# The last stage writes over silu(y) in place; x's first rows come in one load, transposing loads one by one; totals for two weights' scales use a score bank

## The chip, the cores and the metric

The kernel runs on one core of a Trainium2 chip. The core has TensorE for matmuls (its weight loads are shown apart, as PEld), VectorE (DVE), ScalarE (ACT), GpSimd (POOL) and SyncE (SP). In this kernel SyncE issues all DMAs, one after the other. [...] The metric is the device time of one execution in microseconds (us), lower is better.

## The reference

x is 2048 rows of 640 columns. It is normalized by row, and two branches start from the result: sliding-window attention with 32 heads of 20 columns and a window of 256, and an MLP with squared relu and 1536 hidden columns. The output adds x to the product of the attention branch and silu of the MLP branch.

```python
def _A_ref(x, wqkv, wo):
    H = 32; Dh = D // H; W = 256
    qkv = (x @ wqkv).reshape(B, S, 3, H, Dh).transpose(2, 0, 3, 1, 4)
    q, k, v = qkv[0], qkv[1], qkv[2]
    scores = einsum("bhqd,bhkd->bhqk", q, k) * (Dh ** -0.5)
    mask = (idx[:, None] - idx[None, :] >= 0) & (idx[:, None] - idx[None, :] < W)
    p = softmax(where(mask, scores, -1e9))
    o = einsum("bhqk,bhkd->bhqd", p, v)
    return o.transpose(0, 2, 1, 3).reshape(B, S, D) @ wo

def _B_ref(x, w1, b1, w2, b2):
    h = einsum("bsd,df->bsf", x, w1) + b1
    r = where(h > 0, h, 0)
    return einsum("bsf,fd->bsd", r * r, w2) + b2

xn = layernorm(A_x)
out = A_x + _A_ref(xn, A_wqkv, A_wo) * silu(_B_ref(xn, B_w1, B_b1, B_w2, B_b2))
```

(The transposes are written shorter here than in the original; what is computed is the same.)

## The kernel before

**Numbers in two parts.** A float32 operand is split into a float16 high part and a float16 rest, and a product is three matmuls into one PSUM bank: high by high, high by rest, rest by high. Weights are scaled before the split. The scale of a weight comes from its sum of squares: a matmul with a matrix of ones (`totals`, L151) adds over the partitions, a VectorE reduce reads the PSUM result, and a few instructions on single columns (`weight_scale`, L137) make the scale and its inverse.

**Stages.** The first stage normalizes x, turns it (`xT`, four blocks of 512 rows) and makes v. Then 256 steps of attention run: a step is one of 16 pairs of heads (`p`) and one of 16 tiles of 128 rows (`q`). The loop at L1064 has 269 steps, since a step's later parts lag behind: `scores` and `maxima` of step s come with `scores_t` and `exps` of step s-10, `high` of s-11, `low` of s-12 and `values` of s-13. `scores` (L564) fills two banks of tag "s" with up to 320 columns of scores each; the last 128 columns of the first are used every fourth step for a transpose of the row maxima. `maxima` (L577) reads both with VectorE.

**Filler.** Between the parts of a step, `fill` (L1046) takes matmuls from the generator `filler` (L928): the products for the other groups of q and k (`group_unit`, L852), the hidden layer (`hidden_unit`, L877, 8 blocks of 256 rows by 12 groups of 128 columns), the MLP's second product (`out_unit`, L898; `outs` of tag "ysb", stored to `y_d` in DRAM) and at the end the last stage, `out_filler` (L997). All of them take their banks from tag "mm", which has three. `second_scales` (L824) and `out_scales` (L830), the scales of w2 and wo, are called from the filler too; their totals matmul also takes a bank of "mm".

**The last stage.** For each of 8 blocks `u` of 256 rows (two tiles `t` each): `yb` holds y, loaded from `y_d` by `load_y` (L966; two blocks share one buffer of pool `bigp`), and ScalarE makes silu of it in place (L1018). `oT` holds the attention output turned, in two parts, by two transposing loads from `o_d` (`load`, L973), which may start for the blocks 0 and 1 from step 261 on, for 2 and 3 from step 265 on, and for the others when the steps are over. A tile takes two groups of 15 matmuls with wo (`nh`, 320 columns each). `finish` (L998) multiplies the bank by the scale and by silu(y) (L999), adds x (L1000), and after the second group the tile is stored to the output. The result tile `res` has the tag "ysb" with two buffers; that tag is also the one of `outs` in `out_unit`. x's tiles come through `load_res` (L993) into tag "wraw" with three buffers, which the raw pieces of wo use before. A finish runs on VectorE one group later than its matmuls are issued (`pending`, `flush`, L707); stores are collected in `posts` and issued by `post_all` (L696).

**Order.** The order of every engine's instructions, SyncE's DMAs among them, is the order in which this program writes them. A wait of one instruction holds all behind it on the same engine. `bigp` has ten buffers; a new tile takes one whose last users are through.

Of the kernel before, what the change touches and what calls it, by code (L numbers as in the profile page):

```python
# [58 lines left out]
def attn_mlp_kernel(ctx: ExitStack, tc, x, wqkv, wo, w1, b1, w2, b2, out):  # L59
# [69 lines left out]
    def col(name, n=1):  # L129
        return const.tile([P, n], F32, name=name)  # L130
# [19 lines left out]

    def totals(name, r, acc, k=1):  # L151
        nc.tensor.matmul(r, onesf, acc, start=True, stop=True)
        t = col(name, k)
        nc.vector.tensor_reduce(out=t, in_=r.rearrange("p (k n) -> p k n", k=k), op=ALU.add, axis=mybir.AxisListType.X)
        nc.vector.tensor_scalar(t, t, TINY, None, ALU.max)
        return t
# [403 lines left out]
        vps[p] = vp  # L560

    mts = {}

    def scores(p, q, between):  # L564
        i = p % 2
        r = [pat.tile([P, 4 * P], F32, tag="s", name="sps") for h in range(2)]
        rows = between and between(r[0])
        nk = min(WIN + HB, (q + 1) * P)
        for j in range(2):
            q0 = q * P + j * HB  # L570
            k0 = max(0, q0 - WIN)
            for h, ps in enumerate(r):
                rows_ = slice(HB * h, HB * h + HR)
                nc.tensor.matmul(ps[HB * j:HB * (j + 1), :nk], qs[i][rows_, q0:q0 + HB], ks[i][rows_, k0:k0 + nk], start=True, stop=True)  # L574
        return (r, mask if q > 1 else mask0[:, 2 * P - nk:], nk), rows

    def maxima(p, q, r):  # L577
        if q % 4 == 0:
            mts[p, q // 4] = mtp_.tile([P, 8], F32, tag="mt", name="mt")
        mt = mts[p, q // 4]  # L580
        r, mk, nk = r
        for h, ps in enumerate(r):
            junk = mtp_.tile([P, WIN + HB], BF16, tag="junk", name="junk")
            at_ = 4 * h + q % 4
            nc.vector.tensor_tensor_reduce(out=junk[:, :nk], in0=ps[:, :nk], in1=mk, scale=1.0 / MAX_UNIT, scalar=-3.0e38, op0=ALU.add, op1=ALU.max, accum_out=mt[:, at_:at_ + 1])  # L585
        if q % 4 == 3:
            mp = mps[q // 4 % 2]
            v = mp[:, 0:16].rearrange("p (h a b) -> p h a b", h=2, a=2)
            m_ = mt.rearrange("p (h b) -> p h b", h=2)
            nc.gpsimd.tensor_copy(v[:, :, 0, :], m_)  # L590
            nc.gpsimd.tensor_sub(v[:, :, 1, :], m_, v[:, :, 0, :])
            mts[p, q // 4] = mp
# [228 lines left out]
        nc.gpsimd.tensor_mul(g2, ss2, mlp["ic4"])  # L821
        mlp["g2"] = g2

    def second_scales():  # L824
        s2, i2 = weight_scale("w2", totals("w2_t", pmm.tile([P, NF], F32, tag="mm", name="sums2"), mlp["g2"]))
        sf = col("m_sf", NF)
        nc.vector.tensor_scalar(sf, mlp["ic2"], s2, None, ALU.mult)
        mlp.update(s2=sf, i2=i2)

    def out_scales():  # L830
        so, io = weight_scale("wo", totals("wo_t", pmm.tile([P, KC], F32, tag="mm", name="sumso"), sso))
        iw = col("o_inv")
        nc.gpsimd.tensor_mul(iw, io, mlp["iv"])
        nc.gpsimd.tensor_scalar(iw, iw, 1.0 / (XS * V_DOWN), 1.0, ALU.mult, ALU.mult)
        mlp.update(so=so, io=iw)
# [16 lines left out]
    def group_unit(g, b, w):  # L852
        if w == "q":
            if b == 0:
                ensure(f"g{g}")
            if g == 1 and b == 0:
                queue_squares()
            if b == 1 and g + 1 < KC:
                ws[g + 1] = queue_group(g + 1)
            if g == 3 and b == 0:  # L860
                ensure("s")
                weighted_squares()
            if g == 3 and b == 1:
                second_scales()
                for j in range(3):
                    queue_w2(j)
        hi, lo = ws[g][w]
        ps = pmm.tile([P, BT], F32, tag="mm", name="qkps")
        yield from mm_group(ps, [(wt[:, c, :], xT[b][:, part, c, :]) for c in range(KC) for wt, part in ((hi, 0), (hi, 1), (lo, 0))], 0.218)

        def evac():
            hm = stg.tile([P, 2, BT], F16, tag="stg", name="shm")
            qk_parts(hm, ps)
            posts.extend(qk_stores(w, slice(g * P, (g + 1) * P), slice(b * BT, (b + 1) * BT), hm))
        pending.append(evac)
# [51 lines left out]

    def filler():  # L928
        groups = [(group_unit, g, b, w) for g in range(1, KC) for b in range(NB) for w in "qk"]
        hid = [[(hidden_unit, n, fc) for fc in range(NF)] for n in range(nblk)]  # L930
        mlp2 = [[(out_unit, n, tt, nh, third) for tt in range(2) for nh in range(2) for third in range(3)] for n in range(nblk)]
        first = 3 * NB
        units = groups[:first] + merge(groups[first:], hid[0])
        for n in range(nblk - 1):
            units += merge(hid[n + 1], mlp2[n])
        units += mlp2[-1]
        for u in units:
            if u == (hidden_unit, 1, 2):
                out_scales()
            if u[:3] == (hidden_unit, nblk - 1, 0):  # L940
                wo_part = queue_wo()
                for y in range(4):
                    load_y(y)
                shut.add("o")
            if u[:2] == (out_unit, nblk - 1):
                shut.discard("o")
                if u[2:] == (1, 1, 0):
                    ensure("o")
                    load_res(0)
                    load_res(1)  # L950
                for y in range(4, 6):
                    load_y(y)
                for z in range(4):
                    load(z)
            if u == (out_unit, nblk - 1, 1, 1, 2):
                load_y(6)
            yield from u[0](*u[1:])
        ensure("o")
        yield from out_filler(wo_part)
# [30 lines left out]

    xres = {}

    def load_res(t):  # L993
        xres[t] = wgt.tile([P, D], F32, tag="wraw", bufs=RAW, name="xres")
        nc.sync.dma_start(xres[t], x[t * P:(t + 1) * P, :])

    def out_filler(wo_part):  # L997
        def finish(ps, sl, t2, nh, res, xt, t, yb):  # L998
            nc.vector.scalar_tensor_tensor(res[:, sl], ps, mlp["io"], yb[:, t2, sl], ALU.mult, ALU.mult)  # L999
            nc.vector.tensor_add(res[:, sl], res[:, sl], xt[:, sl])  # L1000
            if t == NT - 1:
                post(out[t * P:(t + 1) * P, sl], res[:, sl])
            elif nh:
                post(out[t * P:(t + 1) * P, :], res)

        for u in range(2 * NB):
            while u not in oT:
                load(u)
                if u not in oT:
                    yield None  # L1010
            if u == 0:
                flush()
                post_all()
                load_y(7)
            load(u + 1)
            flush()
            yb = ybs[u]
            nc.scalar.activation(yb, yb, AF.Silu)  # L1018
            for t2 in range(2):
                t = 2 * u + t2  # L1020
                xt = xres.pop(t)
                res = wgt.tile([P, D], F32, tag="ysb", name="res")
                for nh in range(2):
                    sl = slice(nh * HALF, (nh + 1) * HALF)
                    cuts = [sl] if (t, nh) != (NT - 1, 1) else [slice(HALF, HALF + HALF // 2), slice(HALF + HALF // 2, D)]
                    for sl in cuts:
                        ps = pmm.tile([P, HALF], F32, tag="mm", name="wops")[:, 0:sl.stop - sl.start]
                        mms = []
                        for c in range(KC):
                            for op, wp in ((0, 0), (0, 1), (1, 0)):  # L1030
                                mms.append((oT[u][:, op, c, t2 * P:(t2 + 1) * P], wo_part(wp, c)[:, sl]))
                        yield from mm_group(ps, mms, 0.138)
                        if sl is not cuts[-1]:
                            pending.append(lambda ps=ps, sl=sl: finish(ps, sl, t2, nh, res, xt, t, yb))
                    if nh and t + 2 < NT:
                        load_res(t + 2)
                    load(u + 1)
                    load(u + 2)

                    pending.append(lambda args=(ps, sl, t2, nh, res, xt, t, yb): finish(*args))  # L1040

    fl = filler()
    total_ = 8 * (KC - 1) * 15 * 0.218 + 8 * (12 * 15 * 0.111 + 4 * 36 * 0.138)
# [14 lines left out]
    with tc.manual_schedule(engines={E_.PE, E_.Activation, E_.DVE, E_.Pool, E_.SP}):  # L1058
# [5 lines left out]
        for s in range(steps):  # L1064
# [24 lines left out]
            if s % 4 == 1 and 1 < s <= NP * NT + 1:  # L1089
                def between(tp=None, s=s):  # L1090
                    return max_rows((s - 2) // NT, (s - 2) % NT // 4, tp)
# [70 lines left out]
```

## Time and profile before

| | us |
|---|---|
| median of 3 runs | 826.05 (824.84 to 827.02) |
| the profiled execution | 823.97 |
| its span, first to last instruction | 822.2 |
| TensorE busy | 803.9 |
| VectorE busy | 692.4 |
| ScalarE busy | 647.0 |
| GpSimd busy | 496.6 |
| last attention score matmul | about 715 |
| last stage's first matmul | 743.2 |

The profile is one execution. Busy time is that of an engine's own instructions; waiting and DMA issue are not in it. The views used below: the page's shares; the busy time of each engine in chosen stretches of the span (with the clock granted to TensorE, 1.00 is full, the mean busy share of the 16 DMA engines, and what they moved in GB/s); and the timeline of one engine, with start and length of each row in us, the line, the operation, the tiles written and read, their shapes and a count. A bracket at a row's end is the engine's idle time before it and what ended that. SPq is SyncE's queue, where a row is the issue of a DMA and not its transfer. PEld is the loading of matmul weights.

### The profile page before, as it was taken

Reading aid. Unit: us, or ns where it says so; the run is one execution under the profiler, and the core shown is the slowest. Engines: PE = TensorE matmul, PEld = TensorE weight load, DVE = VectorE, ACT = ScalarE, POOL = GpSimd, SP = SyncE. Lnnn points to the kernel's source line nnn. Section 1 sums busy time; section 2 is a strip of 40 time slices with the busy share of each in tenths; the row PEclk is TensorE's granted clock in tenths of the full one; section 3 lists DMA queues with packets and bytes.
Section 4 is the critical chain, followed back from the end, with each engine's and each line's share of the span. In section 5 each row is a group of like instructions: output and inputs, shape, how many; then the busy total and the mean of one; then the engine's idle time right before and its main releaser. Section 6 shows DMA issues by size and latency. Waiting matters only on the chain.

```text
span 822.2 us, 25122 instructions
## 1 busy us (share of the span) xinstructions
PE 803.9 (98%) x9373; PEld 537.0 (65%) x9373; DVE 692.4 (84%) x1943; ACT 647.0 (79%) x1064; POOL 496.6 (60%) x874
## 2 busy tenths in 40 slices
PE   8999999999999999999999999999999999998798
PEld 7775563455555567777777777777777777766476
DVE  6777566898999989999999999999999999982454
ACT  5565455999899989898999999999999999995000
POOL 2000000556687779787888989898897988870000
PEclk9999999999999999999999999999999999999999
DMA  7995358764655522222222222222132261269894
GB/s 249 257 342 165 112 162 263 222 188 123 191 152 151 161 73 55 51 66 67 39 67 60 66 54 68 50 52 70 35 90 52 62 221 41 86 114 201 222 229 158
DMA packets 153250, 104.51 MB, mean 127 GB/s; under 512 B 97192, under 2 KB 127656, under 8 KB 153128
## 3 DMA queue, kind: packets, MB, share of 16 engines
q1 hardware_dynamic: 153128, 102.92, 45.7%
q8 instruction: 73, 1.20, 0.6%
q14 instruction: 49, 0.40, 0.2%
HBM read 60.43 MB, written 36.83 MB: 118 GB/s over the span
## 4 chain that ended last, share of the span: by engine, by line
PE 84%; ACT 6%; DVE 4%; DMA 3%; issue 2%; SPq 1%; ACTq 0%; DVEq 0%
PE hps L718 19%; PE yps L914 19%; PE qkps L718 10%; PE ops L654 8%; PE sps L574 7%; PE wops L718 6%; PE vps L293 6%; PE stps L621 4%; PE qkps L519 3%; ACT p L626 2%; PE tps L257 1%; SPq L980 1%; ACT ph L634 1%; DMA out_dram<-res 1%; DMA y<-ysb 1%
## 5 line engine op out<-in xcount | busy, mean ns | idle before, releaser
L626 ACT ACTIVATE p<-stps,ebias,esc 128x768 f32<-128x768 f32 (+2 forms) x256 | 242.1, 946 | 33.5 <-PE stps L621 16.1
L640 DVE TENSOR_TENSOR pl<-p,ph 128x768 f16<-128x768 f32 (+2 forms) x256 | 247.3, 966 | 2.2 <-ACT ph L634 1.4
L585 DVE CUSTOM_DVE_ANT_0 junk<-sps,mask 128x320 bf16<-128x320 f32 (+2 forms) x512 | 220.4, 466 | 31.3 <-PE sps L574 27.3
L627 POOL TENSOR_SCALAR_AFFINE_SELECT p<-p 128x256 f32<-128x256 f32 x256 | 175.1, 684 | 65.5 <-ACT p L626 57.4
L634 ACT ACTIVATE ph<-p 128x768 f16<-128x768 f32 (+2 forms) x256 | 203.1, 793 | 2.4 <-POOL p L629 1.5
L718 PE MATMUL hps<-xT,w 128*128 128x256 f16 x1440 | 189.5, 273 | 1.0 <-ACT relu L888 1.0
L914 PE MATMUL yps<-w,hh 128*128 128x320 f16 x1152 | 187.1, 300 | 0.0
L718 PEld LDWEIGHTS <-w 128*128 128x128 f16 x1440 | 132.4, 98 | 45.2 <-issue 25.7
L914 PEld LDWEIGHTS <-hh 128*128 128x128 f16 x1152 | 104.8, 98 | 56.2 <-issue 22.5
L718 PE MATMUL qkps<-xT,qkw 128*128 128x512 f16 x480 | 115.5, 380 | 0.0
L629 POOL TENSOR_SCALAR_AFFINE_SELECT p<-p 128x256 f32<-128x256 f32 x224 | 107.0, 478 | 0.0
L654 PE MATMUL ops<-vp,ph 128*128 128x41 f16 x1440 | 89.8, 181 | 0.0
L654 PE MATMUL ops<-vp,pl 128*128 128x41 f16 x1440 | 89.5, 180 | 0.0
L654 PEld LDWEIGHTS <-ph 128*128 128x128 f16 x1440 | 84.6, 96 | 5.1
L574 PE MATMUL sps<-ks,qs 60*64 60x320 f16 (+2 forms) x1024 | 84.0, 313 | 1.7 <-DVE mt L585 1.3
L654 PEld LDWEIGHTS <-pl 128*128 128x128 f16 x1440 | 78.9, 96 | 5.1
L892 POOL TENSOR_TENSOR hh<-sq,hh 128x256 f16<-128x256 f32 x96 | 66.7, 695 | 20.4 <-DVE sq L891 12.2
L621 PE MATMUL stps<-qs,ks 62*64 62x320 f16 (+4 forms) x1024 | 77.5, 290 | 1.0 <-ACT p L626 0.8
L718 PEld LDWEIGHTS <-qkw 128*128 128x128 f16 x480 | 42.4, 98 | 53.7 <-issue 11.5
L590 POOL CAST mp<-mt 128x8 f16<-128x8 f32 x64 | 44.4, 693 | 54.1 <-DVE mt L585 53.4
L718 PE MATMUL wops<-wo,oT 128*128 128x320 f16 (+1 forms) x495 | 67.4, 299 | 7.8 <-DVE res L999 7.8
L293 PE MATMUL vps<-wv,xT 128*128 128x320 f16 x480 | 69.6, 299 | 1.3 <-DVE xT L267 0.4
(150 smaller groups left out, 996.4 us busy)
## 6 DMA issues: line engine op xcount, KB each, us to landing
raw<-in_B_w_dram SPq DMA_DIRECT2D x24, 320.0 KB
ks<-k_d SPq DMA_DIRECT2D x64, 120.0 KB
qs<-q_d SPq DMA_DIRECT2D x64, 120.0 KB
v_d<-vt SPq DMA_DIRECT2D x8, 656.0 KB
vp<-v_d SPq DMA_DIRECT2D x16, 328.0 KB
xt<-in_A_x_dram SPq DMA_DIRECT2D x16, 320.0 KB
k_d<-shm SPq DMA_DIRECT2D x20, 256.0 KB
q_d<-shm SPq DMA_DIRECT2D x20, 256.0 KB
```

What stands on the lines that cost most here:

```text
L293: nc.tensor.matmul(ps, xT[b][:, xp, c, t * P:(t + 1) * P], wv[wp][:, c, nh * HALF:(nh + 1) * HALF], start=n == 0, stop=n == 3 * KC - 1)
L574: nc.tensor.matmul(ps[HB * j:HB * (j + 1), :nk], qs[i][rows_, q0:q0 + HB], ks[i][rows_, k0:k0 + nk], start=True, stop=True)
L585: nc.vector.tensor_tensor_reduce(out=junk[:, :nk], in0=ps[:, :nk], in1=mk, scale=1.0 / MAX_UNIT, scalar=-3.0e38, op0=ALU.add, op1=ALU.max, ...
L621: nc.tensor.matmul(ps[HB * j:HB * (j + 1), hh, c0:c1], ks[i][rows_, kb * P + HB * j:kb * P + HB * (j + 1)], qs[i][rows_, kb * P + c0:kb * ...
L626: nc.scalar.activation(p32[:, :, :n], ps[:, :, :n], AF.Exp, scale=esc[0], bias=ebias)
L627: nc.gpsimd.affine_select(p32[:, :, 0:P], p32[:, :, 0:P], pattern=[[0, 2], [1, P]], compare_op=ALU.is_ge, fill=0.0, base=0, channel_multip ...
L629: nc.gpsimd.affine_select(p32[:, :, 2 * P:], p32[:, :, 2 * P:], pattern=[[0, 2], [-1, P]], compare_op=ALU.is_gt, fill=0.0, base=0, channel ...
L634: nc.scalar.activation(ph[:, :, :n], p32[:, :, :n], AF.Copy)
L640: nc.vector.tensor_sub(pl[:, :, :n], p32[:, :, :n], ph[:, :, :n])
L654: nc.tensor.matmul(ot[:, q % 4, hh, :], t[:, hh, (q - k) * P:(q - k + 1) * P], vp[:, k // 4, k % 4, hh, :], start=m == 1, stop=m == 2 * le ...
L718: nc.tensor.matmul(ps, a, b_, start=j == 0, stop=j == n - 1)
L914: nc.tensor.matmul(ps, hh[:, hp, tt * P:(tt + 1) * P], lin1(w2t, (2 * fc + wp) * D + nh * HALF, HALF), start=fc == 0 and j == 0, stop=fc = ...
```

## The change

Five things change. (1) `finish` writes its result over `yb`, the block that holds silu(y); `res` is now `yb[:, t2]` and no longer a tile of tag "ysb". (2) x's first four tiles come in one load of 512 rows into a buffer of `bigp` (`first_res`), at the start of the last block's second MLP product, instead of four loads of one tile each. (3) From inside the last `out_unit`s only blocks 0 and 1 of `oT` are asked for; in the last stage the block after next is asked for at the second tile of a block only. (4) y's blocks 6 and 7 are loaded at the end of blocks 0 and 1 of the last stage, and the flush and the stores at the start of the stage are left to the usual places. (5) The totals for w2's and wo's scales go into the last 128 columns of the second score bank of the next step: the matmul is issued ahead of that step's scores, and the reduce and what follows it come behind that step's maxima.

```diff
     def totals(name, r, acc, k=1):
         nc.tensor.matmul(r, onesf, acc, start=True, stop=True)
+        return totals_rest(name, r, k)
+
+    def totals_rest(name, r, k=1):
         t = col(name, k)
...
+    sums_due = []
 
     def scores(p, q, between):
         i = p % 2
         r = [pat.tile([P, 4 * P], F32, tag="s", name="sps") for h in range(2)]
         rows = between and between(r[0])
+        sums_rest = sums_due.pop(0)(r[1][:, 3 * P:]) if sums_due else None
...
-        return (r, mask if q > 1 else mask0[:, 2 * P - nk:], nk), rows
+        return (r, mask if q > 1 else mask0[:, 2 * P - nk:], nk, sums_rest), rows
 
     def maxima(p, q, r):
...
+        if sums_rest:
+            sums_rest()
         if q % 4 == 3:
...
-    def second_scales():
-        s2, i2 = weight_scale("w2", totals("w2_t", pmm.tile([P, NF], F32, tag="mm", name="sums2"), mlp["g2"]))
+    def summed(name, acc, rest):
+        def go(r):
+            r = r[:, :acc.shape[-1]]
+            nc.tensor.matmul(r, onesf, acc, start=True, stop=True)
+            return lambda: rest(*weight_scale(name, totals_rest(f"{name}_t", r)))
+        sums_due.append(go)
+
+    def second_scales(s2, i2):
...
-    def out_scales():
-        so, io = weight_scale("wo", totals("wo_t", pmm.tile([P, KC], F32, tag="mm", name="sumso"), sso))
+    def out_scales(so, io):
...
             if g == 3 and b == 1:
-                second_scales()
+                summed("w2", mlp["g2"], second_scales)
...
             if u == (hidden_unit, 1, 2):
-                out_scales()
+                summed("wo", sso, out_scales)
...
             if u[:2] == (out_unit, nblk - 1):
                 shut.discard("o")
-                if u[2:] == (1, 1, 0):
-                    ensure("o")
-                    load_res(0)
-                    load_res(1)
-                for y in range(4, 6):
-                    load_y(y)
-                for z in range(4):
+                if u[2:] == (0, 0, 0):
+                    first_res()
+                    load_y(4)
+                    load_y(5)
+                for z in range(2):
                     load(z)
-            if u == (out_unit, nblk - 1, 1, 1, 2):
-                load_y(6)
             yield from u[0](*u[1:])
...
+    def first_res():
+        rows = bigp.tile([P, SLOT // 2], F32, tag="big", name="xres0").rearrange("p (t d) -> p t d", t=4)
+        nc.sync.dma_start(rows, x[0:4 * P, :].rearrange("(t p) d -> p t d", p=P))
+        for t in range(4):
+            xres[t] = rows[:, t]
...
-        def finish(ps, sl, t2, nh, res, xt, t, yb):
-            nc.vector.scalar_tensor_tensor(res[:, sl], ps, mlp["io"], yb[:, t2, sl], ALU.mult, ALU.mult)
+        def finish(ps, sl, nh, res, xt, t):
+            nc.vector.scalar_tensor_tensor(res[:, sl], ps, mlp["io"], res[:, sl], ALU.mult, ALU.mult)
...
-            if u == 0:
-                flush()
-                post_all()
-                load_y(7)
             load(u + 1)
             flush()
...
-                res = wgt.tile([P, D], F32, tag="ysb", name="res")
+                res = yb[:, t2]
...
-                    if nh and t + 2 < NT:
+                    if nh and 4 <= t + 2 < NT:
                         load_res(t + 2)
                     load(u + 1)
-                    load(u + 2)
-
-                    pending.append(lambda args=(ps, sl, t2, nh, res, xt, t, yb): finish(*args))
+                    if t2:
+                        load(u + 2)
+                    if t2 and nh and u < 2:
+                        load_y(6 + u)
+
+                    pending.append(lambda args=(ps, sl, nh, res, xt, t): finish(*args))
```

More of the change, by code (lines that the diff above doesn't have):

```diff
@@ L580, in maxima @@
         mt = mts[p, q // 4]
-        r, mk, nk = r
+        r, mk, nk, sums_rest = r
         for h, ps in enumerate(r):
@@ L1033, in out_filler @@
                         if sl is not cuts[-1]:
-                            pending.append(lambda ps=ps, sl=sl: finish(ps, sl, t2, nh, res, xt, t, yb))
-                    if nh and t + 2 < NT:
+                            pending.append(lambda ps=ps, sl=sl: finish(ps, sl, nh, res, xt, t))
+                    if nh and 4 <= t + 2 < NT:
                         load_res(t + 2)
                     load(u + 1)
-                    load(u + 2)
-                    pending.append(lambda args=(ps, sl, t2, nh, res, xt, t, yb): finish(*args))
+                    if t2:
[3 more added lines that the diff above has]
+                    pending.append(lambda args=(ps, sl, nh, res, xt, t): finish(*args))
     fl = filler()
```

## The prediction

> **What bounds the kernel now.** I read the page first, for the engine with the largest share and for the chain that ended last.
>
> ```profile
> span 822.2 us, 25122 instructions
> ...
> PE 803.9 (98%) x9373; PEld 537.0 (65%) x9373; DVE 692.4 (84%) x1943; ACT 647.0 (79%) x1064; POOL 496.6 (60%) x874
> ...
> PE 84%; ACT 6%; DVE 4%; DMA 3%; issue 2%; SPq 1%; ACTq 0%; DVEq 0%
> ```
>
> TensorE is busy 98% of the span and is 84% of the chain, so time is to be had only where TensorE stands still: 822.2 - 803.9 = 18.3 us. The view of busy time by stretch says where.
>
> ```profile
> core 0: us, PE busy (x) PEld busy (x) DVE busy (x) ACT busy (x) POOL busy (x), PEclk, DMA share, GB/s
> 310.00:400.00 90.00, 90.00 (x1252) 64.31 (x1248) 85.90 (x254) 84.48 (x135) 77.85 (x134) 1.00 0.25 61
> 713.00:741.00 28.00, 26.98 (x332) 18.99 (x329) 23.47 (x38) 25.86 (x40) 22.30 (x35) 1.00 0.68 150
> 741.00:766.00 25.00, 17.39 (x166) 12.57 (x162) 6.03 (x14) 11.79 (x12) 0.98 (x2) 1.00 0.92 204
> 766.00:822.20 56.20, 52.61 (x390) 37.81 (x389) 29.06 (x58) 0.00 (x0) 0.00 (x0) 0.97 0.77 200
> ```
>
> The middle is full (90.00 of 90). TensorE loses 7.6 us between 741 and 766, where attention ends and the last stage (the product with wo) begins. The timeline of TensorE, without the L654 matmuls of attention, shows the holes; the number in brackets is the idle time before a row and what ended it.
>
> ```profile
> 743.20 1.39 PE L718 MATMUL wops<-wo,oT 128*128 128x320 f16 x9
> 745.03 9.12 PE L718 MATMUL wops<-wo,oT 128*128 128x320 f16 x66
> 756.44 4.24 PE L718 MATMUL wops<-wo,oT 128*128 128x320 f16 x30 [2.28 <-DVE res L999]
> 766.24 52.61 PE L718 MATMUL wops<-wo,oT 128*128 128x320 f16 x390 [5.56 <-DVE res L999]
> ```
>
> Twice TensorE waits for L999, VectorE's multiply that empties a PSUM bank: 2.28 + 5.56 = 7.84 us. So the next question is what L999 waited for, and when SyncE issued that.
>
> ```profile
> 755.83 0.55 DVE L999 SCALAR_TENSOR_TENSOR res<-wops,o_inv,yb 128x320 f32<-128x320 f32 x1 [6.33 <-DMA y<-ysb]
> 765.63 0.55 DVE L999 SCALAR_TENSOR_TENSOR res<-wops,o_inv,yb 128x320 f32<-128x320 f32 x1 [7.73 <-DMA out_dram<-res]
> ```
>
> ```profile
> 742.54 7.43 SPq L980 DMA_TRANSPOSE oT<-o  x4
> ...
> 750.64 0.43 SPq L698 DMA_DIRECT2D y<-ysb  x1
> 755.76 0.32 SPq L971 DMA_DIRECT2D yb<-y  x1
> 756.17 2.19 SPq L698 DMA_DIRECT2D o<-onp  x4
> ...
> 759.84 0.39 SPq L698 DMA_DIRECT2D out_dram<-res  x1
> ```
>
> Both are waits for a buffer. `res` has the tag "ysb" with two buffers. Tile 1's `res` takes the buffer of the last `ysb`, whose store went out only at 750.64, behind four transposing loads that held SyncE for 7.43 us. Tile 2's `res` takes tile 0's, whose store was issued at 759.84, because the load of y at 755.76 first waited for that last store to land and four stores of o stood behind it. The bound in this stretch is a buffer freed by a late store, and SyncE's queue makes the store late.
>
> **The change part by part.** *Results in place.* `res` is now the half of `yb` that holds silu(y), so L999 takes no buffer from "ysb" and both waits lose their object: 7.84 us of idle TensorE. Instruction count and shapes on VectorE stay, so that costs nothing there. The bound above is the whole 7.84; the bound below is 0, if another wait steps in at the same banks. I take 7.84, since nothing else that L999 reads is late: `xres` and `yb` 0 to 5 are loaded before the stage, and ScalarE's silu of five blocks ran far ahead of their use:
>
> ```profile
> 747.08 5.89 ACT L1018 ACTIVATE yb<-yb 128x1280 f32<-128x1280 f32 x5
> ```
>
> *The clock.* After the hole of 5.56 us the granted clock is low; after that of 2.28 it is not.
>
> ```profile
> 757.00:758.00 1.00, 1.00 (x10) 0.73 (x8) 0.86 (x2) 0.00 (x0) 0.00 (x0) 1.00 0.41 113
> 767.00:768.00 1.00, 1.00 (x5) 0.58 (x4) 0.97 (x3) 0.00 (x0) 0.00 (x0) 0.50 0.15 54
> ```
>
> ```profile
> 769.94 0.55 DVE L999 SCALAR_TENSOR_TENSOR res<-wops,o_inv,yb 128x320 f32<-128x320 f32 x1 [1.17 <-PE wops L718]
> ...
> 816.81 0.55 DVE L999 SCALAR_TENSOR_TENSOR res<-wops,o_inv,yb 128x320 f32<-128x320 f32 x1 [0.96 <-PE wops L718]
> ...
> 818.88 0.38 DVE L999 SCALAR_TENSOR_TENSOR res<-wops,o_inv,yb 128x160 f32<-128x160 f32 x1 [0.29 <-PE wops L718]
> ```
>
> From 769.94 to 816.81 there are 23 steps of one group (15 matmuls): 2.04 us each, 0.136 us a matmul. The last stretch holds 24 full groups and two half ones (818.88 - 816.81 = 2.07): 24 x 2.04 + 2.07 = 51.0, where TensorE took 52.61. I leave 0.3 of the difference to the length of the last matmuls and count 1.3 us as slow clock. It goes with the hole (bounds 0.9 and 1.6). [...]
>
> *Totals in a score bank.* Until now the totals matmul took one of three banks "mm". For wo, the next hidden group then had no bank:
>
> ```profile
> 303.21 0.28 PE L152 MATMUL sumso<-ss_o,onesf 128*128 128x5 f32 x2
> 304.54 0.60 PE L718 MATMUL hps<-xT,w 128*128 128x256 f16 x4 [1.05 <-ACT relu L888]
> ```
>
> ```profile
> 304.86 0.15 DVE L154 TENSOR_REDUCE wo_t<-sumso 128x1 f32<-128x5 f32 x1
> ```
>
> ```profile
> 207.86 0.29 PE L152 MATMUL sums<-m_g,onesf 128*128 128x12 f32 x2
> ...
> 208.00 1.89 PE L718 MATMUL qkps<-xT,qkw 128*128 128x512 f16 x8
> ```
>
> For wo 1.05 us go; for w2 TensorE went straight on, so nothing. The added wait is that the score bank stays taken until its reduce is done, some 0.15 us after the maxima, while the next scores come a whole step (over 2 us) later. The five or six small VectorE instructions (about 0.15 us each) move ahead of that step's `low`, which could hold ScalarE's next exponentials by up to 1 us at each of two places; they stood in the same queue before. Bounds: 2 us lost to 1.05 gained. I take 1.05, as the middle is full and passes it on.
>
> *SyncE's order.* The loads of o for blocks 2 and 3 leave the stretch at 742.54 and follow one pair at a time; loads of y 6 and 7 go behind blocks 0 and 1; x's first four tiles come in one load behind the last hidden group. What the new order makes critical is the pair for block 2.
>
> ```profile
> 743.40 0.55 DVE L918 SCALAR_TENSOR_TENSOR ysb<-yps,w_i,b2t 128x320 f32<-128x320 f32 x1 [1.69 <-PE yps L914]
> ...
> 747.21 0.32 DVE L685 TENSOR_TENSOR onp<-on,onp 128x160 f16<-128x160 f32 x1 [1.31 <-ACT onp L681]
> ```
>
> ```profile
> 730.11 6.44 SPq L980 DMA_TRANSPOSE oT<-o  x4
> ```
>
> ```profile
> 732.00:739.00 7.00, 7.00 (x98) 5.09 (x96) 4.71 (x8) 6.22 (x10) 4.21 (x9) 1.00 1.20 188
> ```
>
> The last y store can go at 743.95, the last o store follows VectorE at 747.53, so SyncE comes to block 2's pair near 748.7. Two transposes at 7.43 / 4 = 1.86 take until 752.4. Four that were issued until 736.55 kept the DMA engines full to about 739, so add 2.6: landed at 755. TensorE needs them after 120 matmuls, 111 of them after 745.03: 745.03 + 111 x 0.136 = 760.1. That leaves 5 us, so I cost it at nothing.
>
> *x in one load.* It puts 1.31 MB ahead of y 4 and 5 and of the pieces of wo that ScalarE splits.
>
> ```profile
> 713.19 0.86 SPq L971 DMA_DIRECT2D yb<-y  x2
> ...
> 718.83 0.33 SPq L795 DMA_DIRECT2D raw<-in_A_wo_dram  x1
> ```
>
> ```profile
> 724.12 0.83 ACT L126 ACTIVATE wo<-raw,wo_s 128x640 f16<-128x640 f32 x1
> ```
>
> ```profile
> 717.00:718.00 1.00, 1.00 (x11) 0.62 (x11) 1.00 (x3) 1.00 (x2) 0.92 (x3) 1.00 1.01 411
> ```
>
> At 411 GB/s the 1.31 MB take 3.2 us. The piece of 718.83 is used at 724.12, 5.3 us later, and what lies ahead of it would be through by about 721. Cost 0, at worst 1 us, if it lands after 724.12 and ScalarE, the chain's engine there, stands.
>
> **The sum**: 7.84 + 1.3 + 1.05 = 10.2 us. The profiled execution took 823.97 us, 1.8 outside its span; it would take 813.8. The median shown, 826.05, is 2.1 above it, and would become 815.9 us.
>
> **The rivals.** *The DMA engines fill up.* The shares above give 25 x 0.92 + 56.2 x 0.77 = 66.3 us of DMA time after 741; TensorE without holes needs 743.2 to 809.7, or 66.5. If share were capacity, loads and stores would run as tight as the matmuls, and some pair would be late by 3 to 5 us: 819 to 821. Against it: the share counts packets that wait (1.20 at 188 GB/s, 1.01 at 411), two x tiles less fall in this stretch, and 5 us are spare at the first pair.
>
> *The wait only changes its name.* If block 2's pair landed at 768 in place of 755, TensorE would stand for the same 7.8 us at the same clock loss: 825 to 826, no change. The slowest transposes bound this:
>
> ```profile
> L980 SPq DMA_TRANSPOSE oT<-o x16: 1311/1640/3198, 730.1 to 797.8; - x16
> ```
>
> With two at 3.2 us and a landing as slow as that store's (759.84 to 765.63: 5.8), it lands at 748.7 + 6.4 + 5.8 = 760.9, which is 0.8 late, not 8.
>
> *Slower: a store now blocks the block it reads.* The store of tile t reads `yb` while the next tile's result is written beside it. If the order were kept by whole buffer, every finish would wait for the store before: 5.8 from issue to restart and two multiplies of 0.55 make 6.9 us a tile where TensorE needs 4.08; over some 14 tiles that is 39 us, 855 in all. It decides as soon as a tile takes more than 4.08 + 10.2 / 16 = 4.7 us. Against it stands the last tile, whose first half was still being stored when the other half of the same buffer was written, at 816.81, waiting for TensorE alone:
>
> ```profile
> 815.87 0.33 SPq L698 DMA_DIRECT2D out_dram<-res  x1
> ```
>
> **How the numbers follow.** Forecast 0.76, at 815.9, its own range 813.3 to 818.5 (the bounds of clock and totals, and 1.2 for the scatter of the runs). DMA engines full 0.12, at 820. Wait renamed 0.08, at 826. Slower by the buffer order 0.04, at 855. About 0.3%, 2.5 us, is what a measurement here can tell from no change. Faster holds the first two cases, 0.88; same 0.08; slower 0.04. The range 813.0 to 820.5 holds the forecast and most of the second case.
>
> **What would show it.** Right: TensorE busy without a hole from 743 to its end about 9 us sooner, the granted clock 1.00 throughout the last stage, L999 ended by TensorE alone, no idle time behind the wo totals near 303, the last y store issued near 744. Wrong: TensorE's weight loads idle before block 2 or 3 (a late pair), L999 waiting for a store of out (buffer order), ScalarE idle before L126 near 724 (x's load in the way), or VectorE's small instructions holding the exponentials at the two steps with totals.

## The result and the profile after

The changed kernel takes 815.49 us (median of 4 runs, 814.87 to 817.07) beside 826.53 us for the kernel before: a ratio of 0.9869, 95% interval 0.9842 to 0.9895, or 11 us less. The forecast was 815.9 us in a range of 813.0 to 820.5. The profiled execution took 814.87 us with a span of 813.1, so 9.1 us less than the 822.2 of before.

The page after, its span, its busy times and the chain:

```profile
span 813.1 us, 25102 instructions
...
PE 802.2 (99%) x9373; PEld 537.0 (66%) x9373; DVE 692.8 (85%) x1943; ACT 647.2 (80%) x1064; POOL 496.2 (61%) x874
...
PE 87%; DVE 4%; ACT 4%; DMA 3%; issue 1%; SPq 1%; DVEq 0%; ACTq 0%
```

TensorE's timeline after, the rows of the last stage:

```profile
743.39 1.39 PE L725 MATMUL wops<-wo,oT 128*128 128x320 f16 x9
...
745.22 64.17 PE L725 MATMUL wops<-wo,oT 128*128 128x320 f16 x486
```

One row of 486 matmuls stands where three rows and two holes stood. The stage ran from 743.20 to 818.85 before (75.65 us) and runs from 743.39 to 809.39 now (66.00). The view of who waited for whom (us in total, times, the longest) shows for VectorE's multiplies of the last stage, now L1013, only TensorE:

```profile
DVE yb L1013 <- PE wops L725: 27.8, 30, 1.0
```

SyncE's queue after, where the stage begins:

```profile
744.17 0.34 SPq L705 DMA_DIRECT2D y<-ysb  x1
744.61 3.71 SPq L705 DMA_DIRECT2D o<-onp  x4
748.41 4.18 SPq L988 DMA_TRANSPOSE oT<-o  x2
752.64 0.57 SPq L705 DMA_DIRECT2D out_dram<-yb  x1
```

The last y store goes at 744.17 in place of 750.64, the first result's store at 752.64 in place of 759.84. But the stage's first matmul came no sooner, at 743.39 against 743.20, though the middle is 1.1 us ahead. Something between took it back. The waits of ScalarE and the timelines of ScalarE and TensorE after show what:

```profile
ACT wo L126 <- DMA raw<-in_A_wo_dram: 1.2, 1, 1.2
```

```profile
724.31 0.83 ACT L126 ACTIVATE wo<-raw,wo_s 128x640 f16<-128x640 f32 x1 [1.17 <-DMA raw<-in_A_wo_dram]
```

```profile
726.80 0.33 PE L628 MATMUL stps<-qs,ks 62*64 62x320 f16 x4 [1.41 <-ACT p L633]
```

A piece of wo arrives 1.17 us late behind x's one load, ScalarE stands, and TensorE waits 1.41 us for the exponentials queued behind that piece.

The account of the span, after against before in us: -1.09 up to the last score matmuls of attention (they start at 713.54 after 714.63), the part of the totals; +1.28 from there to the first matmul of the last stage, the part of x's load; -9.65 in the last stage; and +0.36 from the last matmul to the span's end (3.71 after 3.35). Together that is -9.10.

### The profile page after: what moved, and what is told of

Read it like the earlier page. It is cut to its first block, busy times and chain, and to the rows that moved or that the text cites. A ratio compares the mean times of both kernels' runs of the same rounds, so it can differ in the third digit from the quotient of the medians.

```text
span 813.1 us, 25102 instructions
## 1 busy us (share of the span) xinstructions
PE 802.2 (99%) x9373; PEld 537.0 (66%) x9373; DVE 692.8 (85%) x1943; ACT 647.2 (80%) x1064; POOL 496.2 (61%) x874
## 4 chain that ended last, share of the span: by engine, by line
PE 87%; DVE 4%; ACT 4%; DMA 3%; issue 1%; SPq 1%; DVEq 0%; ACTq 0%
PE hps L725 20%; PE yps L926 19%; PE qkps L725 10%; PE wops L725 8%; PE ops L661 8%; PE sps L579 7%; PE vps L296 6%; PE stps L628 4%; PE qkps L522 3%; DMA raw<-in_A_wo_dram 1%; DMA wvr<-in_A_wqkv_dram 1%; PE tps L260 1%; ACT p L633 1%; DMA xres<-in_A_x_dram 1%; DVE junk L590 1%
## 5 line engine op out<-in xcount | busy, mean ns | idle before, releaser
L725 PE MATMUL wops<-wo,oT 128*128 128x320 f16 (+1 forms) x495 | 65.6, 295 | 0.0
```

The costliest lines, as they stand in the source:

```text
L725: nc.tensor.matmul(ps, a, b_, start=j == 0, stop=j == n - 1)
```

## The experiments

All runs, against the kernel before on the same chip; "holes" is what TensorE stood still in the last stage in the profiled execution.

| run | what differs | median us (before) | ratio, 95% interval | span | holes us |
|---|---|---|---|---|---|
| e1_in_place_only | before + result over silu(y) | 822.26 (824.81) | 0.9969 (0.9959 to 0.9980) | 821.7 | 7.03 |
| e2_own_result_tile | changed, but own result tile | 815.29 (824.81) | 0.9883 (0.9866 to 0.9900) | 813.9 | none |
| e3_totals_only | before + totals in score bank | 823.41 (824.81) | 0.9988 (0.9978 to 0.9997) | 822.3 | 2.11 + 3.65 |
| e4_x_later | changed, x's load later | 813.91 (824.81) | 0.9866 (0.9849 to 0.9883) | 811.6 | none |
| e5_y_order_only | before + y loads moved | 816.43 (824.81) | 0.9905 (0.9890 to 0.9920) | 816.2 | 0.54 + 1.94 |
| e6_o_order_only | before + transposing loads moved | 817.68 (824.81) | 0.9914 (0.9899 to 0.9929) | 814.6 | 1.66 |
| e7_x_by_tile | changed, x tile by tile | 813.62 (824.81) | 0.9866 (0.9850 to 0.9883) | 811.9 | none |
| e8_changed_again | the changed kernel | 815.83 (824.81) | 0.9888 (0.9873 to 0.9903) | 812.8 | none |
| e9_order_and_totals | e7, but own result tile | 813.40 (824.40) | 0.9873 (0.9859 to 0.9888) | 811.6 | 0.21 |
| e10_pair_later | e7, transposing pairs one group later | 813.67 (824.40) | 0.9876 (0.9861 to 0.9890) | 811.6 | none |
| e7b_x_by_tile | e7 again | 813.76 (824.40) | 0.9876 (0.9862 to 0.9891) | 811.8 | none |
| e8b_changed_again | the changed kernel | 815.10 (824.40) | 0.9892 (0.9875 to 0.9908) | 813.6 | none |

**Which edit closed the holes: the result in place, or SyncE's order?** First the result in place alone, put into the kernel before.

```diff
-            nc.vector.scalar_tensor_tensor(res[:, sl], ps, mlp["io"], yb[:, t2, sl], ALU.mult, ALU.mult)
+            nc.vector.scalar_tensor_tensor(res[:, sl], ps, mlp["io"], res[:, sl], ALU.mult, ALU.mult)
...
-                res = wgt.tile([P, D], F32, tag="ysb", name="res")
+                res = yb[:, t2]
```

> The kernel before with the result written over silu(y), nothing else changed. Theory A (buffer and SyncE's order both needed): the hole of 2.28 us goes, but x's tile 2 is still issued near 758.4, behind the y load that waits for the last y store, and lands near 762; VectorE's addition for tile 2 stands, the three banks fill, and TensorE stands some 4 to 5 us before 763, with the low clock after it: span near 819, 3 us below before. Rival (the buffer alone made both holes): no hole after 743, span near 812.6, 9.6 us below before.

VectorE's and SyncE's timelines of that run:

```profile
766.60 0.49 DVE L1000 TENSOR_TENSOR yb<-yb,xres 128x320 f32<-128x320 f32 x1 [11.47 <-DMA xres<-in_A_x_dram]
```

```profile
751.53 0.43 SPq L698 DMA_DIRECT2D y<-ysb  x1
757.91 0.32 SPq L971 DMA_DIRECT2D yb<-y  x1
758.33 2.20 SPq L698 DMA_DIRECT2D o<-onp  x4
760.59 1.23 SPq L995 DMA_DIRECT2D xres<-in_A_x_dram  x1
```

The wait for a buffer is gone, and the addition of x one instruction later waits 11.47 us: x's tile 2 stands in the same queue, behind the y load that waits for the last y store. TensorE stands 7.03 us in one piece in place of 7.84 in two. Theory A had the place right and the size too small (4 to 5 us). Measured, the edit alone is worth 0.3%.

Now the other way round: the changed kernel with the result in a tile of its own.

```diff
-            nc.vector.scalar_tensor_tensor(res[:, sl], ps, mlp["io"], res[:, sl], ALU.mult, ALU.mult)
+            nc.vector.scalar_tensor_tensor(res[:, sl], ps, mlp["io"], ybs[t // 2][:, t % 2, sl], ALU.mult, ALU.mult)
...
-                res = yb[:, t2]
+                res = wgt.tile([P, D], F32, tag="ysb", name="res")
```

> The changed kernel with the result in its own tile of two buffers again, all else as changed. Theory A: tile 1 finds its buffer in time, since the last y store goes at 744 now; from tile 2 on every second tile waits for a store of out that stands behind two transposing loads (issued near 752.6, landed near 758.4, wanted at 754.5): VectorE some 4 us late at the even tiles, holes of 0.4 to 1.5 us in TensorE each, 3 to 6 us in all: span 816 to 819. Rival (SyncE's order alone made the gain): no hole, span within 0.5 us of 813.1.

VectorE's waits for the result buffer are back, but TensorE's row has no gap:

```profile
DVE res L1013 <- DMA out_dram<-res: 5.2, 3, 2.2
```

```profile
744.22 1.39 PE L725 MATMUL wops<-wo,oT 128*128 128x320 f16 x9
...
746.05 64.18 PE L725 MATMUL wops<-wo,oT 128*128 128x320 f16 x486
```

Theory A fell: the buffer of two, with stores issued in time, makes VectorE wait at most 2.2 us, and the three banks take that up (a group is 2.04 us). The rival, SyncE's order, holds for the holes. The span, 813.9, is 0.8 us longer than the changed kernel's, and all of that lies ahead of the stage, whose first matmul starts at 744.22 after 743.39; over the runs no loss shows (0.9883 beside 0.9888 and 0.9892 for the changed kernel).

**Which part of the order.** Two runs put one part each into the kernel before.

```diff
-            if u == (out_unit, nblk - 1, 1, 1, 2):
-                load_y(6)
...
-            if u == 0:
-                flush()
-                post_all()
-                load_y(7)
...
+                    if t2 and nh and u < 2:
+                        load_y(6 + u)
```

> The kernel before with only y's loads 6 and 7 moved behind blocks 0 and 1 and the flush and stores at the stage's start left out; result tile, transposing loads, x and totals as before. Theory B (SyncE's order makes the holes, two parts of it one hole each): the last y store still goes near 750, behind four transposing loads, so the first hole of 2 us stays; nothing waits for that store any more, so tile 0's store goes near 753 in place of 759.8 and the second hole goes: span 814.9 to 816. Rival (the buffer of two makes the holes, whatever the order): both holes stay, span near 822.

```diff
-                for z in range(4):
+                for z in range(2):
                     load(z)
...
                     load(u + 1)
-                    load(u + 2)
+                    if t2:
+                        load(u + 2)
```

> The kernel before with only the transposing loads moved (blocks 2 and 3 no longer asked for ahead of the stage, the block after next at a block's second tile). Theory B: the last y store goes near 744, the first hole goes; the load of y 7 still waits for that store and the pair for block 2 now stands ahead of tile 0's store, which lands near 762: a second hole of about 4 us with the low clock after it, span 816.5 to 818.5. Rival (the buffer of two makes the holes, whatever the order): both holes stay, span near 822.

VectorE and TensorE with the y loads moved:

```profile
754.87 0.55 DVE L997 SCALAR_TENSOR_TENSOR res<-wops,o_inv,yb 128x320 f32<-128x320 f32 x1 [4.58 <-DMA y<-ysb]
...
761.05 0.55 DVE L997 SCALAR_TENSOR_TENSOR res<-wops,o_inv,yb 128x320 f32<-128x320 f32 x1 [4.12 <-DMA out_dram<-res]
```

```profile
755.48 4.24 PE L718 MATMUL wops<-wo,oT 128*128 128x320 f16 x30 [0.54 <-DVE res L997]
761.65 51.14 PE L718 MATMUL wops<-wo,oT 128*128 128x320 f16 x390 [1.94 <-DVE res L997]
```

```profile
751.81 0.58 SPq L698 DMA_DIRECT2D y<-ysb  x1
...
755.48 0.38 SPq L698 DMA_DIRECT2D out_dram<-res  x1
```

And with the transposing loads moved, VectorE, TensorE and SyncE:

```profile
759.44 0.55 DVE L999 SCALAR_TENSOR_TENSOR res<-wops,o_inv,yb 128x320 f32<-128x320 f32 x1 [6.05 <-DMA out_dram<-res]
```

```profile
760.04 51.14 PE L718 MATMUL wops<-wo,oT 128*128 128x320 f16 x390 [1.66 <-DVE res L999]
```

```profile
750.63 5.55 SPq L980 DMA_TRANSPOSE oT<-o  x2
756.28 0.53 SPq L698 DMA_DIRECT2D out_dram<-res  x1
```

Both parts alone take most of the gain (0.9905 and 0.9914), and neither closes everything. One hole each, as theory B had it, is only half right. With the y loads moved both holes remain, shorter. The last y store, issued at 751.81, landed within 3.1 us there, where the trace of the kernel before shows 5.1; tile 0's store, issued at 755.48, took 5.6 us until VectorE could go on at 761.05. With the transposing loads moved the first hole goes, as expected, and the second is 1.66 us, not 4: tile 0's store went at 756.28, right behind the pair that held SyncE from 750.63, and VectorE went on 3.2 us later. No low clock follows in either run: in the stretches of five microseconds from 750 to 775 the granted clock is 1.00 in both, and the last 390 matmuls took 51.14 us, where they took 52.61 before. The median with the transposing loads moved is 1.4 us above the profiled execution of that kernel, so its other executions may have stood longer; no trace shows them. The rival (both holes stay, near 822) is out in both runs.

**The totals.**

> The kernel before with only the totals moved to the score bank. Theory: the idle 1.05 us before the hidden group near 304 goes and reaches the end: span 821.1, 1.1 us below before; both holes of the last stage stay. Rival (the small VectorE instructions ahead of low give it back): span 822.2, with 1 us more of waiting of the exponentials or of TensorE in the steps after the totals.

The edit is that of the change, put alone into the kernel before (the functions `totals_rest` and `summed`, and `sums_rest` in `scores` and `maxima`). TensorE's row of the hidden group behind the totals, which waited 1.05 us before, and the row behind the second hole of the last stage:

```profile
303.62 0.60 PE L725 MATMUL hps<-xT,w 128*128 128x256 f16 x4
```

```profile
765.15 53.79 PE L725 MATMUL wops<-wo,oT 128*128 128x320 f16 x390 [3.65 <-DVE res L1011]
```

The idle 1.05 us is gone. The matmuls just ahead of that place start 0.41 us later than in the kernel before (302.93 after 302.52), and the last score matmuls 0.68 us earlier (713.95 after 714.63): 1.09 us gained in between, as much as in the changed kernel. The runs are 1.4 us faster in the median (ratio 0.9988, 0.9978 to 0.9997, so 0.2 to 1.8 us). The span of the single profile hides it, since its last stage fell worse: holes of 2.11 and 3.65 us, and the low clock after each (the last section has the first; behind the second the granted clock was 0.50 from 765 to 770, and 390 matmuls took 53.79 us).

**x in one load.** The changed kernel with that load at another place, or with none.

```diff
+                if u[2:] == (0, 1, 1):
+                    first_res()
                 if u[2:] == (0, 0, 0):
-                    first_res()
                     load_y(4)
```

> The changed kernel with x's one load issued four units later, behind the last two pieces of wo. Theory (the load crowds the pieces of wo out): ScalarE's wait of 1.2 us for a piece of wo goes, TensorE's idle 1.41 us near 726 goes, span near 811.8, 1.3 us below the changed kernel. Rival (the pieces are late by the two y loads or by themselves): the wait stays, span 813.1. Second rival (the load now delays the transposing loads issued from 730 on): a new hole before the last stage's first matmul, span 813 to 816.

```diff
+                if u[2:] == (1, 1, 0):
+                    ensure("o")
+                    load_res(0)
+                    load_res(1)
                 if u[2:] == (0, 0, 0):
-                    first_res()
                     load_y(4)
...
-                    if nh and 4 <= t + 2 < NT:
+                    if nh and t + 2 < NT:
```

> The changed kernel with x loaded tile by tile at the old places, all else as changed. Theory: no hole in the last stage, since SyncE is free in time for tiles 2 and 3, and ScalarE's wait of 1.2 us for a piece of wo goes: span near 811.8, as with x's one load issued later. Rival (x in one load is needed to keep VectorE's additions fed): VectorE waits for x at tiles 2 or 3 and a hole of 1 us or more opens between 750 and 765, span 813 or more.

> The changed kernel with x tile by tile once more, beside the changed kernel in the same runs: 1 to 2 us below it, span near 811.9.

> The changed kernel once more, for its time beside the others on one chip: span 813 to 815, ScalarE waiting about 1.2 us for a piece of wo, no hole in the last stage.

> The changed kernel once more: span 812.5 to 814, ScalarE waiting 0.7 to 1.2 us for a piece of wo.

ScalarE's fourth piece of wo, with x's load later, with x by tile, and in the changed kernel once more:

```profile
722.97 0.83 ACT L126 ACTIVATE wo<-raw,wo_s 128x640 f16<-128x640 f32 x1
```

```profile
723.41 0.83 ACT L126 ACTIVATE wo<-raw,wo_s 128x640 f16<-128x640 f32 x1
```

```profile
723.97 0.83 ACT L126 ACTIVATE wo<-raw,wo_s 128x640 f16<-128x640 f32 x1 [0.68 <-DMA raw<-in_A_wo_dram]
```

The wait goes when the load goes or moves, and comes back with it (1.17, 0.68 and 1.03 us in three profiles of the changed kernel; about 1.2 was expected of the second). In runs side by side on one chip, x by tile took 813.45 to 813.98 us where the changed kernel took 814.48 to 815.88, and again on another chip 813.51 to 813.96 against 814.86 to 815.33: 2.2 and 1.3 us between the medians. From the last score matmuls to the first matmul of the last stage it is 29.85 us in the changed kernel, 28.58 with x by tile (713.92 to 742.50) and 28.57 in the kernel before. x in one load is a small loss at its place, and the additions don't need it: with x by tile VectorE waits 0.25 us for x once, and TensorE never.

**What is needed at all.** The last two start from x by tile. One takes the result in place out again:

```diff
-            nc.vector.scalar_tensor_tensor(res[:, sl], ps, mlp["io"], res[:, sl], ALU.mult, ALU.mult)
+            nc.vector.scalar_tensor_tensor(res[:, sl], ps, mlp["io"], ybs[t // 2][:, t % 2, sl], ALU.mult, ALU.mult)
...
-                res = yb[:, t2]
+                res = wgt.tile([P, D], F32, tag="ysb", name="res")
```

> The kernel before with SyncE's new order of the y loads and the transposing loads and the totals in the score bank; result in its own tile of two buffers, x tile by tile. Theory C (the order makes the gain, the buffer of two is then enough): VectorE waits 1 to 2.5 us for a store of out at some tiles, three banks take it up, no hole in TensorE, span 811.5 to 812.5. Rival (writing in place is needed for part of it): holes of 0.5 us or more after 750, span 813 to 816.

```profile
DVE res L1016 <- DMA out_dram<-res: 17.2, 8, 3.1
```

```profile
743.52 25.43 PE L725 MATMUL wops<-wo,oT 128*128 128x320 f16 x186
769.15 39.09 PE L725 MATMUL wops<-wo,oT 128*128 128x320 f16 x300 [0.21 <-DVE res L1016]
```

Eight waits for the result buffer, 17.2 us on VectorE, cost TensorE 0.21 us. At 813.40 us this is the shortest median, 0.4 us below x by tile with the result in place, which their spread doesn't tell apart. So the order of the loads and the totals carry the whole gain; writing in place is spare room here.

The other asks how near a late transposing pair is:

```diff
-                    if t2:
+                    if t2 and nh:
                         load(u + 2)
```

> The changed kernel with x tile by tile, and with the transposing pair for the block after next asked for one group (2 us) later. Theory (the pair for block 2 has about 5 us to spare, later pairs more): no hole, span 811.5 to 812.5. Rival (the DMA engines are nearly full and the pairs land just in time): TensorE's weight loads stand before block 2 or later ones, holes of 1 to 3 us, span 813 to 820.

```profile
749.49 4.47 SPq L991 DMA_TRANSPOSE oT<-o  x2
```

The pair for block 2 went out at 749.49, 1.4 us later than with x by tile alone (748.06). No hole opened, and the median is 813.67 us. So at this pair at least 1.4 us were to spare; how much more, no run shows.

## Why the prediction was right, point by point

*The bound.* Right. The gain came from the stretch where TensorE waited for VectorE, VectorE for buffers, and the buffers for stores that stood behind other DMAs in SyncE's queue.

*Results in place: 7.84 us.* The amount was right, and it was put to the wrong edit. The step was: `res` takes no buffer, so both waits lose their object, and nothing else that is read is late. In place alone left a hole of 7.03 us, because x's tile 2 stood in the same queue. The new order, with the buffers of before, left no hole in one run and 0.21 us in another. So the step held only because the change also reorders the queue; that x's tiles come ahead in one load was not needed for it. The lower bound, "another wait steps in", was what e1 measured.

*The clock: 1.3 us.* A term a little too small: without the low clock the same 390 matmuls took 51.14 us in place of 52.61 in two runs, so the slow stretch cost 1.47. In all the last stage became 1.8 us shorter beside the holes. The other 0.3 go with the restarts after the holes, which the sum had not counted: at a granted clock of 1.00 486 matmuls took 64.17 us in one row in the changed kernel, and the three rows of the kernel before, the last at its length without the low clock, give 9.12 + 4.24 + 51.14 = 64.50.

*Totals: 1.05 us.* Right: 1.09 by two traces, 1.4 in the medians of the edit alone. The small VectorE instructions that moved cost nothing that shows.

*SyncE's order: cost nothing.* Right for the pair for block 2: issued at 748.41 where 748.7 was worked out, and issued at 749.49 it still did no harm. What the step missed is that this order was itself the gain.

*x in one load: cost 0, at worst 1 us.* Wrong in the size. The step took what lies ahead of wo's piece to be through by about 721, at the rate of one full microsecond (411 GB/s); ScalarE could start on the piece only at 724.31. The same stretch in the kernel before, and in two windows of the changed kernel:

```profile
714.00:724.00 10.00, 9.47 (x126) 6.60 (x125) 9.48 (x17) 9.97 (x16) 9.68 (x14) 1.00 0.81 231
```

```profile
714.00:719.00 5.00, 4.93 (x61) 3.43 (x60) 5.00 (x11) 5.00 (x8) 4.68 (x8) 1.00 1.02 406
719.00:724.00 5.00, 4.47 (x56) 3.16 (x54) 4.48 (x8) 4.14 (x6) 5.00 (x7) 1.00 0.94 309
```

Before, 2.3 MB moved in these 10 us at a DMA share of 0.81. With x's load it was 2.0 MB to 719 and 1.5 after it, 3.6 in all, at shares of 1.02 and 0.94: the 1.3 MB of x came on top, and the engines had little time free until 724. TensorE lost 1.3 us by it. Why the rate fell behind 719 was not tried.

With 0.4 more at the end and 0.5 more gained in the last stage, 10.2 forecast became 9.1 in the profiled spans.

*The rivals.* DMA engines full: against it stands the window of the last stage after, TensorE busy for 65.00 of 65 us at a DMA share of 0.88.

```profile
744.00:809.00 65.00, 65.00 (x513) 47.48 (x512) 33.58 (x68) 9.12 (x9) 0.99 (x2) 1.00 0.88 226
```

A renamed wait did not appear in the changed kernel, but it is just what e1 shows when the order stays as it was. Of the order by whole buffer nothing shows: no multiply waits for a store.

*How close the number came.* This is in part luck. The edit that did the work, SyncE's order, stood in the bundle at no price, and the edit that had its price was spare; the sum came out because it was read off the holes and the bundle had both. And 815.9 lies 0.4 us from the measured 815.49, while the gain behind it, 10.2 us, was 9.1 in the profiled spans and 9.0 and 9.3 in the later medians on two chips (824.81 to 815.83, 824.40 to 815.10). The 11.0 between the first medians rests on four runs of the kernel before that lie between 824.84 and 828.48. The forecast's own range, 813.3 to 818.5, does not come out of the bounds that it names: a clock of 0.9 to 1.6 us, totals between 2 lost and 1.05 gained, and 1.2 of scatter give 814.4 to 820.5.

## What to carry to other kernels

When an engine waits for a buffer, look at the queue that should free it before adding or saving buffers: here stores stood behind four transposing loads (7.43 us of SyncE's time) and behind a load that waited for a store (the store issued at 750.64, the load at 755.76), and reordering closed both holes, but for 0.21 us, with the old buffers. The edit that removes the named wait need not be the one that brings the gain, so each edit of a bundle is to be tried alone and left out. A load issued early is not free if a later, more urgent one queues behind it: here a piece of wo came 1.17 us late behind x's load, and the span was 1.28 us longer by it.

## What was not expected of the hardware

A hole of 2.11 us brought the low clock too. In the kernel before a hole of 2.28 us left the granted clock at 1.00; with the totals alone, the one of 2.11 us was followed by three microseconds at 0.50, from 757 to 760; the first of them:

```profile
755.59 5.91 PE L725 MATMUL wops<-wo,oT 128*128 128x320 f16 x30 [2.11 <-DVE res L1011]
```

```profile
757.00:758.00 1.00, 1.00 (x5) 0.55 (x4) 0.05 (x1) 0.00 (x0) 0.00 (x0) 0.50 0.98 389
```

30 matmuls took 5.91 us there where they took 4.24 before. The granted clock also went to 0.50 with the holes of 3.65 us (totals alone), 5.56 us (the kernel before) and 7.03 us (result in place alone), and stayed at 1.00 with those of 1.94 us (y loads moved) and 1.66 us (transposing loads moved). So from the length of a hole alone these traces don't tell whether the low clock comes: 2.11 us had it and 2.28 us had not. What else decides was not tried.

The issue of transposing loads held SyncE for very different times: two took 3.28 us from 787.78 in the kernel before, and up to 6.93 in the changed one:

```profile
763.27 6.93 SPq L988 DMA_TRANSPOSE oT<-o  x2
```

What sets that length was not tried.
